# The first DFT of the last two x tiles by column block, and the order of the moves behind it

## The chip, the core and the metric

The kernel runs on one core of one Trainium2 chip. The metric is the device time of one execution in microseconds (us). The page of the profile and its trace come from one profiled execution of their own; its span runs from the first to the last instruction.

## The reference

Two layers follow each other on `x` of 4096 rows by 640 columns, both scaled and shifted by vectors made from `c` (`mod = silu(c) @ w_mod`, six vectors of 640). The change lies in the first layer, a spectral one; the second, a gated feed-forward layer with F = 1728, follows it in the same program.

```python
h = layernorm(x) * (1 + ca) + sa
X = rfft2(h)                     # along the 4096 rows: 2049 frequencies
z = X.reshape(..., 4, 160)       # 4 blocks of 160 columns
hr = relu(zr @ w1[0] - zi @ w1[1] + b1[0]);  hi = relu(zi @ w1[0] + zr @ w1[1] + b1[1])
o_r = hr @ w2[0] - hi @ w2[1] + b2[0];       o_i = hi @ w2[0] + hr @ w2[1] + b2[1]
y = irfft2(softshrink(o_r + 1j * o_i, 0.01))
x = x + ga * y
h = layernorm(x) * (1 + cb) + sb
x = x + gb * ((silu(h @ w_gate) * (h @ w_up)) @ w_down)
```

All is float32.

## The kernel before, in words

The 4096 rows are taken as 128 x 32 (`n1` on the partitions, `n2` in a tile's rows). The FFT is done in two steps of matrix products.

**First DFT, along n1.** Eight tiles `xa0` to `xa7` hold four values of `n2` each (128 partitions, 4 x 640). For each tile `ln_stats` (L379) takes mean and variance on VectorE and the inverse root on GpSimd, `ln_apply` (L390) normalizes the four rows, some on ScalarE and some on VectorE, `dft_a` (L408) multiplies with the constant `fa` on TensorE, and `evac_a` (L418) copies the products from PSUM back into `xa`. A product of 128 x 512 covers either one row's first 128 columns of all four blocks (`i` = 0 to 3) or the last 32 columns of all blocks and rows (`i` = 4, the remainder columns); they land in `xa[:, i, 0:512]` and `xa[:, :, 512:640]`. The loop at L431 runs these steps for t = 0 to 7, software pipelined: statistics two tiles ahead, normalization one.

**The turn through DRAM.** `moves` (L356) writes the tile to DRAM with `write_s1(t, f)` (L345), where f names which frequencies: f = 0 holds chunks 0 and 1 (32 of the 128 partitions, 320 KB), f = 1 chunks 2 and 3 (320 KB), f = 2 the last four chunks (640 KB). `load_g(ch)` (L301) reads a chunk back with `n2` on the partitions: `g` of chunk `ch`, 128 partitions (4 n2 + q) by 4 x 640, in four DMAs, one for each q. The first chunk is read in two parts: rows n2 < 28 from GpSimd's queue, the last four from SyncE's (SP's) queue after tile 7 is written. All other moves named here go through SP's queue, in program order; a DMA that waits there holds all behind it.

**Second DFT and the two layers, by chunk.** Eight chunks `ch` with four blocks `b` each make 32 steps p = 4 ch + b (L806). For a block, `stage_b(ch, t)` (L547, eight matmuls) makes the spectrum of columns 128 t to 128 t + 127 out of `g`; t = 0 to 3 are the blocks' first 128 columns, t = 4 the remainder columns of all four. `evac_b` (L555) splits a product into a high part (ScalarE) and a low part (VectorE), tile `z`; for chunk 0 `evac_r` (L568) does the same with the remainder columns of a block, tile `rz`. For later chunks the remainders go through DRAM: `rem_high`, `rem_low`, `rem_move`, `rem_read` (L600 to L622). `stage_l1` (L624) is the first complex layer, `tail_l1` (L661) its last part, `stage_l2` (L669) the second layer, `stage_i` (L729) the inverse step. In step p come `stage_l1(p)`, the `stage_b` of a later block, `stage_l2` of p - 1, `stage_i` of p - 7.

PSUM has eight banks: two each for the tags p1, p2, p3, and single ones b0 and b1. `stage_b` takes b0, for t = 4 b1 (L549); `stage_l2` takes p2. The bank b1 with chunk 0's remainders is read by `evac_r` of all four blocks, so `stage_b(1, 4)` can start only when the last of them is done.

**The weights.** `load_weights` reads raw w1 or w2 (two DMAs of 640 KB, `rm` and `rr`), `prep_weights` lists the jobs, `weights_high` (L278) rounds a weight to its high part and `weights_low` (L284, VectorE) makes the low part. For w1 the high parts are ScalarE's (L448), for w2 GpSimd's (L478). `first_scale` (L403) and `columns` (L316) make the vector `ca1` = 1 + ca; `idle(n)` (L324) issues 2 n small matmuls that compute nothing that is used.

**Memory.** The tiles of the pool `p2` (L468: w2a, w2b, w2c, tt and others) lie where the `xa` tiles lay, so each waits until the writes of the tile under it are done. Before the steps, L453 to L462 issue the second chunk's load, the writes of tiles 0 and 4 to 7 for f = 1, the third chunk's load, and those for f = 2.

The order is written out by hand: each engine runs its instructions in program order, and only semaphores hold it.

## Time and profile before

| | us |
|---|---|
| time, median of 3 runs | 1468.21 (1466.46 to 1470.22) |
| the profiled execution, its own time | 1461.29 |
| its span on the page | 1459.5 |
| TensorE busy in the span | 1416.4 |
| VectorE busy | 1083.6 |
| ScalarE busy | 785.5 |
| GpSimd busy | 551.7 |

The profiled execution was 6.92 us faster than the median of the three runs beside it. In the rows of the trace a timeline line gives start, length, engine, line of the kernel, operation, tiles written and read, shapes and a count; in brackets stands how long the engine was idle before it and what released it. PE is TensorE, PEld its weight loads, DVE VectorE, ACT ScalarE, POOL GpSimd, SPq SyncE's queue; for SPq and for DMA rows on POOL the length is that of the issue, not of the transfer.

### The profile page before, as it was taken

The page shows a single profiled execution, that of the slowest core. Times are in us where ns is not written, and L with a number is a line of the kernel's source. Part 1 is how long each engine was busy: PE and PEld are TensorE (multiplying, and loading weights), DVE is VectorE, ACT ScalarE, POOL GpSimd, SP SyncE. Part 2 cuts the span into 40 slices and gives each one's busy share as a digit, 9 for nine tenths or more (in the row PEclk, how much of TensorE's full clock was granted, in tenths as well). Part 3 has the DMA queues.
Part 4 walks back from the last instruction along what each step waited for, and adds up shares of the span by engine and source line. Part 5 has one row for each costly group of instructions (what it writes and reads, how often), then busy time and mean ns, then how long its engine had stood idle before and what let it go on. Part 6 is the DMA issues. An engine that isn't in the chain of part 4 may idle for free.

```text
span 1459.5 us, 24171 instructions
## 1 busy us (share of the span) xinstructions
PE 1416.4 (97%) x8628; PEld 1341.4 (92%) x8628; DVE 1083.6 (74%) x1963; ACT 785.5 (54%) x1554; POOL 551.7 (38%) x646
## 2 busy tenths in 40 slices
PE   6999999998999999999999999999999999999998
PEld 2799999966888888899999999999999999999998
DVE  8568877878797788757887768888747767567775
ACT  7658888744545555544565446555434444244432
POOL 5400100044655444322544424444324545046532
PEclk9999999999999999999999999999999999999999
DMA  9967767648677988798987997877696666966652
GB/s 379 338 215 228 232 199 219 220 145 275 235 276 267 337 293 279 274 364 291 314 271 248 342 367 254 310 246 249 237 345 219 222 215 238 352 212 232 205 188 83
DMA packets 184712, 380.07 MB, mean 260 GB/s; under 512 B 22480, under 2 KB 103056, under 8 KB 182544
## 3 DMA queue, kind: packets, MB, share of 16 engines
q1 hardware_dynamic: 176080, 360.99, 71.8%
q0 software_dynamic: 6928, 14.91, 3.3%
q10 hardware_dynamic: 1584, 2.62, 0.5%
q8 instruction: 68, 1.11, 0.3%
q14 instruction: 52, 0.43, 0.1%
HBM read 263.91 MB, written 105.39 MB: 253 GB/s over the span
## 4 chain that ended last, share of the span: by engine, by line
PE 61%; DVE 8%; DMA 4%; issue 2%; ACT 2%; POOL 1%; SPq 0%; POOLq 0%; DVEq 0%; ACTq 0%
PE pd L2269 12%; PE pw L1950 8%; PE pw L1948 8%; PE pw L1949 8%; PE pd_X L2129 4%; PE pg L1813 2%; PE pg L1812 2%; PE pg L1814 2%; PE pd_Y L2129 2%; PE pw L1959 2%; PE pw L1960 2%; PE pw L1961 2%; DMA cr<-s 2%; DVE wb L1266 2%; PE pd_Z L2129 1%
## 5 line engine op out<-in xcount | busy, mean ns | idle before, releaser
L2269 PE MATMUL pd<-wdh,a 128*128 128x320 f32 x1040 | 238.9, 310 | 1.5 <-DVE a L1849 1.3
L2269 PEld LDWEIGHTS pd<-wdh,a 128*128 128x128 f32 x1040 | 176.2, 188 | 2.5 <-DVE a L1849 1.6
L1266 DVE TENSOR_TENSOR wb<-r,wb 128x512 fp32r<-128x512 f32 (+3 forms) x156 | 159.8, 1032 | 16.3 <-ACT wb L1263 14.0
L2269 PE MATMUL pd<-wdl,a 128*128 128x320 f32 x540 | 166.3, 309 | 0.0
L1948 PE MATMUL pw<-h,wt 128*128 128x384 f32 x416 | 140.8, 339 | 3.1 <-ACT s_x L1967 2.1
L1950 PE MATMUL pw<-h,wt 128*128 128x384 f32 x416 | 140.4, 338 | 0.0
L1949 PE MATMUL pw<-h,wt 128*128 128x384 f32 x416 | 139.9, 336 | 0.0
L1263 ACT ACTIVATE wb<-r 128x512 fp32r<-128x512 f32 (+3 forms) x172 | 117.9, 703 | 32.8 <-PE pw L1961 24.8
L2241 DVE TENSOR_TENSOR x<-x,pd 128x320 f32<-128x320 f32 x240 | 108.9, 477 | 35.7 <-PE pd L2269 32.1
L1950 PE MATMUL pw<-h,wb 128*128 128x384 f32 x312 | 105.1, 337 | 2.3 <-DVE wb L1266 2.3
L1948 PE MATMUL pw<-h,wb 128*128 128x384 f32 x312 | 105.5, 338 | 0.0
L1949 PE MATMUL pw<-h,wb 128*128 128x384 f32 x312 | 105.0, 337 | 0.0
L1812 PE MATMUL pg<-ht,wb 128*128 128x512 f32 x260 | 102.8, 396 | 1.3 <-ACT wb L1263 1.3
L1814 PE MATMUL pg<-ht,wb 128*128 128x512 f32 x260 | 101.7, 391 | 2.2 <-DVE wb L1266 2.2
L2269 PEld LDWEIGHTS pd<-wdl,a 128*128 128x128 f32 x540 | 101.4, 188 | 0.5
L1813 PE MATMUL pg<-ht,wb 128*128 128x512 f32 x260 | 101.5, 390 | 0.0
L742 POOL DMA_DIRECT2D s<-co x28 | 15.5, 555 | 190.8 <-ACT co L741 183.0
L1967 ACT ACTIVATE s_x<-pw 128x384 f32<-128x384 f32 x52 | 25.4, 489 | 113.6 <-PE pw L1950 112.9
L1525 POOL TENSOR_TENSOR cr<-cr,gab 128x640 f32<-128x640 f32 x28 | 47.5, 1696 | 100.5 <-DMA cr<-s 89.6
L1948 PEld LDWEIGHTS pw<-h,wt 128*128 128x128 f32 x416 | 78.3, 188 | 4.7 <-ACT s_x L1967 3.1
L1949 PEld LDWEIGHTS pw<-h,wt 128*128 128x128 f32 x416 | 78.3, 188 | 0.0
L1950 PEld LDWEIGHTS pw<-h,wt 128*128 128x128 f32 x416 | 78.3, 188 | 0.0
(335 smaller groups left out, 4079.0 us busy)
## 6 DMA issues: line engine op xcount, KB each, us to landing
wt<-td SPq DMA_DIRECT2D x104, 512.0 KB, 5.3
hs<-ho SPq DMA_DIRECT2D x52, 512.0 KB, 5.5
h<-hs SPq DMA_DIRECT2D x32, 768.0 KB, 7.9
r<-in_B_w_gate_dram SPq DMA_DIRECT2D x36, 640.0 KB, 4.8
r<-in_B_w_up_dram SPq DMA_DIRECT2D x36, 640.0 KB, 5.0
wdr<-wdd SPq DMA_DIRECT2D x21, 640.0 KB, 5.2
td<-wt SPq DMA_DIRECT2D x25, 512.0 KB, 6.0
g<-s SPq DMA_DIRECT2D x28, 320.0 KB, 5.9
```

What stands on the lines that cost most here:

```text
L1263: act.activation(wbs[t, n][:, 0, ks, e], raw[t, n][:, ks, e], AF.Copy)
L1266: (pool if onp else dve).tensor_tensor(wbs[t, n][:, 1, ks, e], raw[t, n][:, ks, e], f32(wbs[t, n][:, 0, ks, e]), op=OP.subtract)
L1525: pool.tensor_tensor(crs[r], crs[r], gab, op=OP.mult)
L1812: mm(b, wh, hh, start=(kk == 0), stop=False)
L1813: mm(b, wh, hl, start=False, stop=False)
L1814: mm(b, wl, hh, start=False, stop=(kk == 4))
L1948: mm(b, w(0, kp), a[:, kp, 0], start=start and kp == 0, stop=False, skip_group_check=not start)
L1949: mm(b, w(0, kp), a[:, kp, 1], start=False, stop=False, skip_group_check=not start)
L1950: mm(b, w(1, kp), a[:, kp, 0], start=False, stop=kp == 1, skip_group_check=not start)
L2129: mm(bk[b, i][:, :320], x, y, start=new and j == 0, stop=j == len(seq) - 1, skip_group_check=not new)
L2241: dve.tensor_tensor(x2[:, e], x2[:, e], x[0][:, :320], op=OP.add)
L2269: mm(pd[g, hf][0][:, :320], l, m, start=i == 0, stop=i == len(s) - 1 and not (last and len(gs) > 1))
```

## The change

The tiles 0 to 5 go as before. For tiles 6 and 7 the DFT is taken by column block (`dft_c`, `evac_c`): product i < 4 holds block i's first 128 columns of all four rows, i = 4 the remainder columns, which now go to a tile `rst` of their own. Block 0 and the remainders of both tiles come first, are written (`first`) and read back for chunk 0; the other three blocks (`rest`) follow, with the raw weights w2 and the writes of tiles 2 and 3 for f = 1 and 2 between. All rows of tile 7 are normalized on VectorE, and three of tile 6. The high parts of w1 are made between the evacuations, `idle(54)` becomes `idle(14)`. Each part of `load_g` is one DMA instead of four. The other writes for f = 1 and 2 wait behind a small DMA (`s1h`) that reads the second chunk's tile. In the steps, only `stage_b(0, 0)` and `stage_b(0, 4)` stand ahead of the loop; blocks 1 and 2 come in step 0, block 3 in step 1. The high part of w2b moves from GpSimd to ScalarE (step 0), the low parts of w2 to the ends of step 0 and the middle of step 1, and chunk 1's `rem_move` and `rem_read` from SP's queue to GpSimd's.

```diff
-            def load_g(ch, lo=0, hi=32, dma=None):
+            def load_g(ch, lo=0, hi=32, dma=None, cols=(slice(0, D),)):
...
-                for q in range(4):
-                    (dma or nc.sync).dma_start(gs[ch][4 * lo + q:4 * hi:4], src[q, lo:hi])
+                for e in cols:
+                    (dma or nc.sync).dma_start(gs[ch][4 * lo:4 * hi, :, e], src[:, lo:hi, :, e].rearrange("q n j d -> n q j d"))
...
+                def write_s1(t, f, cols=None, dma=None):
+                    r = slice((0, 2, 1)[f], 128, (4, 4, 2)[f])
+                    if t < 6:
+                        (dma or nc.sync).dma_start(s1[f][:, 4 * t:4 * t + 4, :], xas[t][r])
+                        return
+                    for e in cols or (slice(0, 512), slice(512, 640)):
+                        (dma or nc.sync).dma_start(s1[f][:, 4 * t:4 * t + 4, e], rst[t][r] if e.start == 512 else xas[t][r, :, e])
...
-                        raws[2] = load_weights(rp, w2, "2")
-                    elif t < 7:
-                        if t == 6:
-                            load_g(0, 0, 28, pool)
+                    elif t == 4:
                         for f in (1, 2):
-                            write_s1(t - 3, f)
-                    else:
-                        load_g(0, 28, 32)
+                            write_s1(1, f)
+                    elif t == 5:
+                        load_g(0, 0, 20, pool)
...
-                        if i >= (4, 2, 2, 3, 2, 3, 2, 3)[t]:
+                        if i >= (4, 2, 2, 3, 2, 3, 1, 0)[t]:
...
+                def dft_c(t, i):
+                    xnr = xas[t].rearrange("p a (b e) -> p a b e", b=NB)
...
+                    mm(pa, fa, xnr[:, :, i, 0:128] if i < 4 else xnr[:, :, :, 128:160], start=True, stop=True)
+                    pas[t, i] = pa
+
+                def evac_c(t, i, eng=None):
+                    if i == 4:
+                        o = rst[t] = low_p.tile([P, 4, 128], F32, tag="e", bufs=2, name=f"rst{t}")
+                    else:
+                        o = xas[t][:, :, 128 * i:128 * i + 128]
+                    v = pas[t, i].rearrange("p (a e) -> p a e", a=4)
+                    if eng:
+                        eng.tensor_copy(o, v)
+                    else:
+                        act.activation(o, v, AF.Copy)
...
+                ln_apply(7)
+                for q in ((6, 0), (6, 4), (6, 1), (7, 0), (7, 4)):
+                    dft_c(*q)
+                evac_c(6, 0)
+                evac_c(6, 4)
+                evac_c(6, 1)
+                first_scale(0, 3)
+                evac_c(7, 0, dve)
+                evac_c(7, 4, dve)
+                first = (slice(0, 128), slice(512, 640))
+                rest = (slice(128, 512),)
+                write_s1(6, 0, first)
+                write_s1(7, 0, first)
+                load_g(0, 20, 32, None, first)
+                raws[2] = load_weights(rp, w2, "2")
+                for q in ((6, 2), (6, 3), (7, 1), (7, 2), (7, 3)):
+                    dft_c(*q)
+                jobs = prep_weights(raws[1], w1a, w1b, w1c, True)
...
+                for job in jobs[:3]:
+                    weights_high(*job)
+                evac_c(6, 2)
+                evac_c(6, 3)
+                evac_c(7, 1)
+                for job in jobs[3:6]:
+                    weights_high(*job)
+                evac_c(7, 2)
+                evac_c(7, 3)
+                for job in jobs[6:]:
+                    weights_high(*job)
+                write_s1(6, 0, rest)
+                write_s1(7, 0, rest)
+                for f in (1, 2):
+                    write_s1(2, f)
+                load_g(0, 20, 32, None, rest)
+                for f in (1, 2):
+                    write_s1(3, f)
+
+                first_scale(3, 5)
                 remainders(acc0, wx0)
                 pm1 = columns(acc0, wx0)
+                idle(14)
+                for job in jobs[:4]:
+                    weights_low(*job)
                 dve.tensor_scalar(ca1, pm1[:, 0:5], 1.0, None, op0=OP.add)
-                idle(54)
-                for job in prep_weights(raws[1], w1a, w1b, w1c, True):
-                    weights_high(*job)
+                for job in jobs[4:]:
                     weights_low(*job)
...
-            for t in (0, 4, 5, 6, 7):
-                write_s1(t, 1)
+            nc.sync.dma_start(s1h, gs[1][127:128, 3, 0:16])
+            for f in (1, 2):
+                for t in (0, 4, 5, 6, 7):
+                    write_s1(t, f)
             load_g(2)
             load_tb(2)
-            for t in (0, 4, 5, 6, 7):
-                write_s1(t, 2)
...
-            for job in prep2:
-                weights_high(*job, pool)
+            prep2 = [prep2[k] for k in (0, 3, 1, 4, 2, 5)]
+            for n, job in enumerate(prep2):
+                if n // 2 != 1:
+                    weights_high(*job, pool)
+            pool.dma_start(bm.rearrange("p a b c -> p (a b c)"), k_bm)
...
-                pb = bank0(1 if t == 4 else 0, [P, 2, 256], f"pb{ch}_{t}")
+                pb = (ps.tile([P, 2, 256], F32, tag="p2", name=f"pb{ch}_{t}") if (ch, t) in ((0, 1), (0, 3)) else
+                      bank0(1 if t == 4 else 0, [P, 2, 256], f"pb{ch}_{t}"))
...
-                nc.sync.dma_start(rzd[ch, :, :, 0:NN], f32(rts[ch].rearrange("p l i k -> p (l i) k")[:, :, 0:NN]))
+                (pool if ch == 1 else nc.sync).dma_start(rzd[ch, :, :, 0:NN], f32(rts[ch].rearrange("p l i k -> p (l i) k")[:, :, 0:NN]))
...
-            for b in range(3):
-                stage_b(0, b)
-                if b == 0:
-                    stage_b(0, 4)
-                evac_b(0, b)
-                evac_r(0, b)
-                if b == 1:
-                    idle(8)
-            for job in prep2[:3]:
-                weights_low(*job)
+            stage_b(0, 0)
+            stage_b(0, 4)
+            evac_b(0, 0)
+            evac_r(0, 0)
...
-                if b == 0:
+                if p < 2:
+                    todo = ([(0, 1), (0, 2)], [(0, 3), (1, 4), (1, 0)])[p]
+                elif b == 0:
                     todo = [(ch, 3)]
...
                     if q[1] < 4:
                         evac_b(*q)
+                        if q[0] == 0:
+                            evac_r(*q)
                 for f, *a in sums.get(p, ()):
                     f(*a)
-
                 if p == 0:
-                    evac_rh(0, 3)
+                    for job in prep2[2:4]:
+                        weights_high(*job)
+
+                if p == 1:
+                    for job in prep2[3:]:
+                        weights_low(*job)
...
-                if p == 0:
-                    evac_rl(0, 3)
...
                 if p == 0:
-                    for job in prep2[3:]:
+                    for job in prep2[:3]:
                         weights_low(*job)
```

33 lines of the change are left out of this document (16 added, 17 removed).

## The prediction, made before the change was run

> **What bounds the kernel now.** I read the page first, then the busy time in stretches, then TensorE's timeline of the first 110 us.
>
> ```profile
> span 1459.5 us, 24171 instructions
> PE 1416.4 (97%) x8628; PEld 1341.4 (92%) x8628; DVE 1083.6 (74%) x1963; ACT 785.5 (54%) x1554; POOL 551.7 (38%) x646
> ...
> 84.46:1459.50 1375.04, 1347.76 (x8302) 1296.04 (x8300) 1022.20 (x1800) 729.42 (x1454) 515.69 (x573) 1.00 0.75 255
> ...
> 63.60:84.46 20.86, 17.61 (x130) 17.23 (x131) 15.86 (x28) 12.37 (x26) 3.51 (x4) 0.92 0.78 298
> ```
>
> In a row of a stretch stand its length, the busy time of PE, PEld, DVE, ACT and POOL, the granted clock, the DMA share and GB/s. From 84.46 us on TensorE is busy for 98% of the time: whatever brings that point forward is kept to the end. The change acts before it.
>
> ```profile
> 31.24 17.74 PE L415 MATMUL pa<-xa,fa 128*128 128x512 f32 x40 [1.81 <-ACT xa L397]
> 49.67 1.05 PE L320 MATMUL pmc<-ones,acc 128*128 128x1 f32 x8 [0.69 <-ACT xa L426]
> 50.80 12.30 PE L327 MATMUL pz<-ones 128*128 128x128 f32 x108
> 63.61 2.02 PE L552 MATMUL pb<-tb,g 128*128 128x128 f32 x16 [0.50 <-DMA g<-s]
> ...
> 72.51 1.05 PE L552 MATMUL pb<-tb,g 128*128 128x128 f32 x8
> 74.11 0.40 PE L639 MATMUL pl<-rz,w1c 128*128 128x256 f32 x2
> ...
> 75.78 0.28 PE L652 MATMUL pl<-rz,w1c 128*128 128x256 f32 x1
> 78.63 3.22 PE L552 MATMUL pb<-tb,g 128*128 128x128 f32 x16 [2.56 <-DVE rz L592]
> 84.46 0.52 PE L639 MATMUL pl<-z,w1a 128*128 128x256 f32 x3
> 89.02 0.60 PE L685 MATMUL pc<-w2a,h 128*128 128x320 f32 x3
> 90.20 0.52 PE L639 MATMUL pl<-z,w1a 128*128 128x256 f32 x3
> 104.62 1.95 PE L552 MATMUL pb<-tb,g 128*128 128x128 f32 x16
> ```
>
> The last DFT ends at 31.24 + 17.74 = 48.98. Then TensorE multiplies nothing of use for 12.3 us (L327 is `idle`) and waits for `g`: the second DFT starts at 63.61. A second hole, 2.56 us, waits for VectorE's `rz` (bank b1). Step 2 starts at 84.46, step 3 at 90.20. So two stretches count: the trip through DRAM, and the chain from the first `stage_b` to step 2, 20.85 us long.
>
> **The trip through DRAM.**
>
> ```profile
> 39.30 11.77 SPq L346 DMA_DIRECT2D s<-xa  x10
> 54.54 5.46 SPq L309 DMA_DIRECT2D g<-s  x8
> ...
> 52.32 2.64 POOL L309 DMA_DIRECT2D g<-s  x4 [11.45 <-DMA s<-xa]
> ...
> xx<-tt SPq DMA_DIRECT2D x12, 160.0 KB, 3.0
> ...
> rzd<-rt SPq DMA_DIRECT2D x2, 512.0 KB, 6.1
> ...
> DMA to landing us min/median/max: 3.3/6.1/6.9
> ...
> 45.00:50.00 5.00, 4.31 (x13) 1.83 (x12) 0.98 (x2) 4.16 (x9) 0.00 (x0) 1.00 0.96 399
> ```
>
> Before, the last write goes out just before 51.07; the last load waits for its landing until 54.54 and lands some 6 us after its issue (the line "to landing" is of L309), because the DMA engines are full (share 0.96). The change takes 1.31 MB of raw weights and two of three 0.98 MB writes out of the queue ahead of that point: 3.3 MB, at 0.40 MB per us 8 us of transfers, so by 43 us the queue has run empty.
>
> ```profile
> 40.20 0.61 DVE L395 TENSOR_SCALAR xa<-xa,mv_a,rs_a 128x640 f32<-128x640 f32 x1 [0.93 <-POOL rs_a L197]
> 41.31 3.65 DVE L406 SCALAR_TENSOR_TENSOR acc<-wm,sc,acc 128x640 f32<-128x640 f32 x4
> 49.02 1.29 DVE L422 COPY xa<-pa 128x512 f32<-128x512 f32 x2 [4.06 <-PE pa L415]
> ...
> 40.73 2.10 ACT L426 ACTIVATE xa<-pa 128x512 f32<-128x512 f32 x4
> ```
>
> *Ends of the DFT.* 20 products in 17.74 us are 0.887 each; the last ten start at 40.1 and end at 48.98 in either order, the fifth (tile 7's remainders) at 44.6. ScalarE has one 128x640 pass less (about 0.8) ahead of tile 5's five copies and ends them at 42.5, not 43.3; three copies of 2.10 / 4 are done at 44.1. VectorE normalizes tile 7 from 40.2 (four times 0.54, to 42.4), adds three terms of `first_scale` (0.55 and two of 0.91, to 44.7) and copies two products (1.29): 46.0. TensorE keeps 48.98, as all this lies beside it; so do w1's high parts, twelve passes of at most 0.63 (a row below) and about 5 us in all, done by 52 and wanted after 55.
>
> *First part.* The last write is issued at 46.1, against 50.6 (51.07 less one issue). An empty queue lands a small DMA in about 3.0 (row of xx), so at 49.1; the two loads are issued at 49.1 and 49.7 (5.46 / 8 = 0.68 each) and land by 52.7 to 53.0 (3.0 to 3.3). TensorE: the columns from 49.0 (1.1 us), then 28 matmuls of 12.30 / 108 = 0.114: 3.2, so it is free at **53.4**, and that is the first `stage_b`, 10.2 us earlier. The load is covered by `idle` with 0.4 to 0.7 us to spare; past that each us late costs one.
>
> *Second part.* On SP's queue the weights follow at 50.3, then two writes `rest` (0.39 MB), (2, 1) and (2, 2), 0.98 MB. At 0.42 MB per us from 51.6 the weights end at 54.7, `rest` at 55.7 and lands at 56.7. Only then does SP issue the load of `rest`; behind 2.3 us of writes, to 58.0, its 0.29 MB land at about **60.0** (3.3 after the issue, the minimum of L309's row). Bounds: 59.3, the end of these transfers, and 66, if the write's landing takes the 3.5 of before (51.07 to 54.54) and the load the crowded 6.9. I take the near end, since the ring is emptier. TensorE wants it 5.85 us after its first `stage_b`: two of them 2.02, ScalarE's and VectorE's `rz` 1.9 (rows below), and what of `stage_l1` follows its first product with `rz`, 1.8 (74.11 to 75.9). That is 59.3, so it is late by 0.7.
>
> That a load of some columns waits for those columns alone: the trace lets ScalarE write strided columns of `w1a` while VectorE has not yet written the others that the program lists earlier.
>
> ```profile
> 52.81 0.63 ACT L282 ACTIVATE w1a<-rm 128x512 fp32r<-128x512 f32 x1
> ...
> 53.01 0.29 DVE L285 SCALAR_TENSOR_TENSOR w1a<-rm,w1a 128x128 fp32r<-128x128 f32 x1
> ```
>
> **The chain from `stage_b(0, 1)` to step 2.** This is where the change gives back.
>
> ```profile
> L592 DVE SCALAR_TENSOR_TENSOR rz<-pb,ca,rz 32x256 fp32r<-32x256 f32 x8 | 3.9, 483 | 0.9 <-ACT rz L582 0.8
> L560 DVE SCALAR_TENSOR_TENSOR z<-pb,ca,z 128x512 fp32r<-128x512 f32 x5 | 3.7, 747 | 11.2 <-ACT z L559 11.2
> ...
> L285 DVE SCALAR_TENSOR_TENSOR w2b<-rm,w2b 128x640 fp32r<-128x640 f32 x2 | 1.6, 818 | 0.0
> L644 DVE TENSOR_TENSOR h<-h,h 128x256 fp32r<-128x256 f32 x4 | 1.5, 419 | 0.0
> L657 DVE SCALAR_TENSOR_TENSOR u<-pl,b1r,u 64x256 f32<-64x256 f32 x2 | 1.0, 476 | 0.1
> ...
> L665 DVE SCALAR_TENSOR_TENSOR r<-u,r 64x256 fp32r<-64x256 f32 x2 | 0.8, 418 | 0.1
> ...
> L559 ACT ACTIVATE z<-pb,ca 128x512 fp32r<-128x512 f32 x12 | 8.3, 689 | 16.8 <-PE pb L552 16.8
> L582 ACT ACTIVATE rz<-pb,ca 32x256 fp32r<-32x256 f32 x8 | 3.7, 467 | 0.3 <-PE pb L552 0.2
> ...
> L722 ACT ACTIVATE xh<-xx 128x640 fp32r<-128x640 f32 x3 | 2.2, 729 | 0.0
> ```
>
> Before, blocks 0 to 2 were split while TensorE idled. Now, from 60.0: block 1 on TensorE 1.05, to 61.1. ScalarE: z and rz of blocks 1 and 2, two times 0.69 + 2 x 0.47, to 64.4 with overlaps; the two high parts of w2b, not shown on ScalarE, by the same shape in L722 0.73 each (bounds 0.69, the smaller z, and 1.8, POOL's), to 65.8; the tail of `stage_l1(0)`, as long as VectorE's (L665), to 66.2. VectorE: its tail 0.42; three low parts of w2, 0.75 pipelined, to 68.9; the low parts of `stage_l1(1)` (L644 twice, L657, pipelined) 1.15; z and rz of block 3, 0.75 + 0.97, to 71.8. Only now is b1 free for `stage_b(1, 4)`: TensorE has stood from about 66.5, 5.3 us. With `stage_b(1, 0)` that takes 3.22 at the slow rate of 78.63 (bounds 1.95, row of 104.62, and 3.9, twice that): 75.0. z(1, 0), which the program puts ahead of the last low parts: ScalarE 0.69, VectorE 0.75, 76.5; three low parts of w2, 2.3, to 78.8; the last product and the second half of `stage_l2(0)` (89.02 to 90.20, 1.18) 1.5: step 2 starts at **80.4**. Against 84.46 that is 4.0 us less, and counted the other way: 10.2 won, 5.85 + 20.4 - 20.85 = 5.4 given back in the longer chain, 0.7 to the late second part.
>
> The other edits cost nothing while covered. POOL's w2a and w2c wait for raw weights and for the writes of tile 3, which land by 62 (0.98 MB behind the load of `rest`); they are needed from 66.6 and 77. The second chunk, 1.31 MB behind those, lands near 66, wanted at 71.8. The bulk writes behind `s1h`, 4.9 MB or 11.7 us, free the memory of tt by 77, wanted at 79. Chunk 1's remainders on POOL's queue are issued at 80.5; nothing is queued behind them there until step 7. A landing of 6.1 (row of rzd), four issues of 0.68 and a landing of 3.0 to 3.3 end near 92, wanted at 93.
>
> **The clock.**
>
> ```profile
> 80.00:81.00 1.00, 1.00 (x7) 0.50 1.02 401
> 82.00:83.00 1.00, 1.00 (x7) 0.65 1.05 442
> ```
>
> The third number from the end is the granted clock: after the hole of 2.56 us it stood at 0.50 and came back within the stretch 82 to 83. That is in the 3.22 above. A second such stretch may follow the 2 us of waiting inside `stage_l2(0)`; on three us of work it costs some 1.5 and leaves 2.5 of the 4.0 (1465.7, within the forecast's range). I take none, since that wait is shorter than the one that the trace shows. The Trainium skill, "TensorE: Matmul & The Clock Gate", section "HAM oscillation", gives as a rule that gaps of more than some 3.4 us slow the clock. The trace has it after 2.56, so the measurement decides; by that page the new 5.3 us hole costs one slow stretch and the 2 us could not bring a second.
>
> **The rivals.** (a) No slow clock, second part in time: 0.7 and 1.3 less, 78.4, 6.0 us gained: 1462.2. For it: the slow window may fall into the hole. (b) The second part lands 2 to 4 us later, at 62 to 64: the gain shrinks to 2 to 0, about 1467.2. For it: 1.31 MB of weights lie right ahead of it. (c) Slower: the second part lands at 66, its upper bound, because its write and its load each wait in a queue that the weights and (2, f) have filled. The gain is gone from 64.0 on; at 66 step 2 starts at 86.4, and TensorE, having stood for 6 us ahead of block 1, pays another slow stretch of 1.7: 3.6 us slower, 1471.8. Against it: the queue is empty at 49. (d) The change doesn't do what it says: `stage_b(0, 0)` waits for both parts. Then the first `stage_b` is at 60.0 and step 2 follows 5.85 + 20.4 later: 86.3, 1.8 us slower, 1470.0. The two rows of w1a speak against it.
>
> **How the numbers follow.** The profiled execution takes 1461.29; 4.0 less is 1457.3. The median of the runs is 1468.21, 6.9 above it; I predict on that: **1464.2**. Forecast 0.46 (a gain of 2 to 5), (a) 0.20, (b) 0.14, (c) 0.15, (d) 0.05. The range leaves out a tenth on each side: 1460.0 (gain of (a), and 2 us of spread of the runs, 1466.46 to 1470.22) to 1472.0 (case (c)). The forecast's own range is 1463 to 1466.5. A measurement of this kernel can tell about 0.3%, 4.4 us, from no change. Faster by more: all of (a) and 0.21 of the forecast, 0.41. Slower by more: 0.08 of (c), 0.02 of (d) and 0.02 of the rest, 0.12. Within: 0.47.
>
> **What would show it.** In the profile after: `pz` 28 matmuls long and the first `stage_b` near 53.4; the second near 60, released by DMA g; a hole of 5 us before `stage_b(1, 4)`, released by DVE rz; step 2 near 80.4; after it TensorE as busy as before. A first `stage_b` beyond 55, a second beyond 64, or TensorE waiting for `rz` by DMA in step 4 would make the prediction wrong.

## The result and the profile after

The changed kernel takes 1472.58 us (median of 17 runs), the kernel before 1466.46 (17 runs beside them): **1.0043 times as long, 95% interval 1.0032 to 1.0054**, some 6 us slower. Predicted were 1464.2, 4.0 less than the 1468.21 it started from. The profiled execution takes 1473.94 us. Executions of one kernel differ by several us (the 17 of before ran from 1461.96 to 1470.22), so the start is compared below by the traces and the whole by the ratios.

"Step n" is the n-th pass of the main loop; it begins with its first product `pl<-z,w1a`. First the page of after and its busy time in stretches (length; busy PE, PEld, DVE, ACT, POOL; granted clock; DMA share; GB/s).

```profile
span 1472.1 us, 23954 instructions
PE 1415.9 (96%) x8532; PEld 1338.0 (91%) x8532; DVE 1082.6 (74%) x1967; ACT 782.5 (53%) x1552; POOL 549.9 (37%) x646
```

```profile
90.52:1472.10 1381.58, 1350.81 (x8301) 1296.94 (x8300) 1018.65 (x1798) 728.08 (x1454) 518.61 (x578) 1.00 0.74 253
55.55:90.52 34.97, 23.15 (x115) 21.69 (x115) 16.53 (x29) 13.72 (x28) 8.92 (x8) 0.70 0.96 343
```

From step 2 on TensorE is as busy as before (98%), though the stretch lasts 6.5 us longer than in the profiled execution of before (1375.04 us). The stretch ahead of it grew from 20.86 to 34.97 us, with more than 11 us of holes and a mean clock of 0.70 instead of 0.92. TensorE's timeline shows the holes, in brackets with what ended them:

```profile
49.74 3.37 PE L328 MATMUL pz<-ones 128*128 128x128 f32 x28
55.55 3.51 PE L615 MATMUL pb<-tb,g 128*128 128x128 f32 x16 [2.44 <-DMA g<-s]
...
67.18 3.78 PE L615 MATMUL pb<-tb,g 128*128 128x128 f32 x16 [3.98 <-DMA g<-s]
...
80.37 3.75 PE L615 MATMUL pb<-tb,g 128*128 128x128 f32 x16 [4.97 <-issue]
...
90.52 0.84 PE L702 MATMUL pl<-z,w1a 128*128 128x256 f32 x3
...
97.53 0.51 PE L702 MATMUL pl<-z,w1a 128*128 128x256 f32 x3
```

The three lines L615 begin with `stage_b` of (0, 0), of (0, 1) and of (1, 4); each holds a second one, (0, 4), (0, 2) and (1, 0). For the hole of 4.97 us the profile names no releaser; VectorE's `rz` of block 3 ends at 80.27, 0.1 us ahead, and e4 below shows that it is the bank. Beside the prediction:

| start of, us | before | predicted | after |
|---|---|---|---|
| first `stage_b` | 63.61 | 53.4 | 55.55 |
| `stage_b(0, 1)` | 66.30 | 60.0 | 67.18 |
| step 2 | 84.46 | 80.4 | 90.52 |
| step 3 | 90.20 | 86.1 | 97.53 |
| step 5 | 102.10 | 98.0 | 109.01 |

(Predicted steps 3 and 5 are 80.4 and the length that the steps had before.) Step 5 is 6.9 us late, and the medians differ by 6.1. The two profiled executions differ by another 5.7 us behind step 5: from there to the end of the span it takes 1357.4 us in before and 1363.1 in after. The kernel before shows both values by itself: a second trace of it (e12) has 1358.0, and e16, changed only ahead of the first `stage_b`, 1363.1. So three terms are to be explained: the second part (7.2 us later than predicted), the chain behind it (23.3 us instead of 20.4) and step 2 itself (7.0 instead of 5.7). The issues on the DMA queues between 42 and 53 us, and then between 54 and 70 us (number, KB of one, median us from issue to landing):

```profile
g<-s POOLq DMA_DIRECT2D x1, 800.0 KB, 9.6
...
s<-xa SPq DMA_DIRECT2D x2, 64.0 KB, 8.7
s<-rst SPq DMA_DIRECT2D x2, 64.0 KB, 7.6
```

```profile
rm<-in_A_w_dram SPq DMA_DIRECT2D x1, 640.0 KB, 4.3
rr<-in_A_w_dram SPq DMA_DIRECT2D x1, 640.0 KB, 6.4
...
s<-xa SPq DMA_DIRECT2D x2, 192.0 KB, 6.4
```

The first part's four writes (64 KB each) took up to 8.7 us to land, not 3.0, and those of the second part 6.4. The load on GpSimd's queue landed at 52.1 (issued at 42.47), the last of the four writes at 52.6. Meanwhile the DMA engines were far from full. The last column but one is their share, first in the kernel before, then in after; the work that didn't run between 44 and 56 us keeps them full until 96:

```profile
44.00:48.00 4.00, 4.00 (x11) 1.74 (x10) 0.93 (x2) 4.00 (x8) 0.00 (x0) 1.00 1.01 425
48.00:52.00 4.00, 3.31 (x23) 2.48 (x22) 2.44 (x6) 3.15 (x7) 0.00 (x0) 1.00 0.92 383
52.00:56.00 4.00, 4.00 (x38) 4.00 (x37) 4.00 (x11) 3.08 (x10) 3.60 (x6) 1.00 0.84 271
...
92.00:96.00 4.00, 4.00 (x33) 4.00 (x32) 2.72 (x6) 2.46 (x6) 0.00 (x0) 1.00 0.61 141
```

```profile
44.00:48.00 4.00, 4.00 (x11) 1.85 (x10) 3.93 (x7) 3.56 (x9) 0.00 (x0) 1.00 0.74 181
48.00:52.00 4.00, 4.00 (x33) 3.52 (x32) 3.90 (x10) 3.65 (x10) 0.00 (x0) 1.00 0.55 135
52.00:56.00 4.00, 1.56 (x13) 1.40 (x13) 0.95 (x4) 0.00 (x0) 0.00 (x0) 0.98 0.26 63
...
92.00:96.00 4.00, 4.00 (x30) 4.00 (x29) 1.30 (x3) 2.67 (x7) 0.00 (x0) 0.83 1.03 339
```

### The profile page after: what moved, and what is told of

Read it like the earlier page. It is cut to its first block, busy times and chain, and to the rows that moved or that the text cites. A ratio compares the mean times of both kernels' runs of the same rounds, so it can differ in the third digit from the quotient of the medians.

```text
span 1472.1 us, 23954 instructions
## 1 busy us (share of the span) xinstructions
PE 1415.9 (96%) x8532; PEld 1338.0 (91%) x8532; DVE 1082.6 (74%) x1967; ACT 782.5 (53%) x1552; POOL 549.9 (37%) x646
## 4 chain that ended last, share of the span: by engine, by line
PE 61%; DVE 6%; DMA 5%; issue 2%; ACT 2%; POOL 2%; SPq 0%; ACTq 0%; POOLq 0%; DVEq 0%
PE pd L2332 12%; PE pw L2013 8%; PE pw L2011 8%; PE pw L2012 8%; PE pd_X L2192 4%; PE pg L1875 2%; PE pg L1876 2%; PE pg L1877 2%; PE pd_Y L2192 2%; PE pw L2022 2%; PE pw L2024 2%; PE pw L2023 2%; DMA hs<-ho 2%; DMA cr<-s 2%; PE pd_Z L2192 1%
## 5 line engine op out<-in xcount | busy, mean ns | idle before, releaser
L2013 PEld LDWEIGHTS pw<-h,wt 128*128 128x128 f32 x416 | 78.1, 188 | 0.0
```

Of the source, the lines that this page charges most:

```text
L2013: mm(b, w(1, kp), a[:, kp, 0], start=False, stop=kp == 1, skip_group_check=not start)
```

## The experiments

**Theories.** *Moves*: the first part's writes wait for chunk 0's load of 20 rows, the second's for the raw weights ahead of them. *Chain*: from `stage_b(0, 1)` on, VectorE's order and bank b1 set the pace. Rivals: GpSimd's queue, or pieces of 512 bytes, are slow by themselves; TensorE's halved clock is the cause. Later came a fourth theory, *dates*: the bulk transfers set a date further on, so that what is won at the start is lost there. e1 to e4, e8, e9 and e11 change one thing in the changed kernel (e11 besides has e1's edit); e7 starts from the kernel before. All ratios are to the kernel before, run beside them. By their whole time none of e1 to e4, e6, e8 and e9 can be told from the changed kernel (1.0032 to 1.0054); what each term costs is read from the traces, one execution each. e13 and e18 lie below its interval.

| kernel | first `stage_b` | `stage_b(0, 1)` | step 2 | step 5 | ratio (95%) |
|---|---|---|---|---|---|
| e1, load on SP | 56.31 | 68.22 | 90.4 | 108.1 | 1.0054 (1.0039 to 1.0069) |
| e2, 16 rows | 52.97 | 64.32 | 86.9 | 105.3 | 1.0060 (1.0044 to 1.0077) |
| e3, weights behind | 56.65 | 64.38 | 86.2 | 106.7 | 1.0040 (1.0024 to 1.0055) |
| e4, other bank | 56.08 | 67.77 | 86.5 | 106.5 | 1.0041 (1.0025 to 1.0056) |
| e6 = e2 + e3 + e4 | 52.67 | 59.78 | 79.1 | 103.0 | 1.0030 (1.0018 to 1.0042) |
| e7, before, moves alone | 59.23 | 61.93 | 80.6 | 105.8 | 1.0041 (1.0028 to 1.0055) |
| e8, no early load | 53.38 | 66.17 | 89.5 | 108.3 | 1.0042 (1.0028 to 1.0056) |
| e9, holes filled | 56.84 | 69.00 | 90.9 | 109.9 | 1.0066 (1.0045 to 1.0088) |
| e10 = e7 + bulk writes first | 58.93 | 61.85 | 81.6 | 100.6 | 1.0007 (0.9997 to 1.0017) |
| e11, 17 rows | 77.73 | 89.82 | 113.2 | 131.6 | one run, 1489.84 us |
| e12, before again | 63.62 | 66.31 | 84.5 | 102.5 | 1.0006 (0.9992 to 1.0021) |
| e13 = e6 without `s1h` | 53.06 | 59.53 | 78.1 | 102.3 | 1.0014 (0.9998 to 1.0030) |
| e14, before, other bank | 64.17 | 66.86 | 83.0 | 103.1 | 0.9997 (0.9982 to 1.0011) |
| e15 = e10 + other bank | 59.53 | 62.23 | 78.8 | 101.9 | 0.9996 (0.9982 to 1.0010) |
| e16, before, started later | 69.37 | 72.00 | 90.2 | 108.1 | 1.0030 (1.0018 to 1.0042) |
| e17 = e15, chunk 2 later | 59.77 | 63.39 | 80.2 | 102.3 | 1.0006 (0.9989 to 1.0024) |
| e18 = e13, chunk 2 later | 53.73 | 59.94 | 79.0 | 102.1 | 1.0003 (0.9983 to 1.0023) |
| e19 = e15, chunk 2 on POOL | 59.08 | 61.77 | 79.6 | 100.5 | 0.9990 (0.9974 to 1.0006) |

(In e7, e10, e12, e14 to e17 and e19, built on the kernel before, the block (0, 1) is the third `stage_b` and follows the first at once.)

**The first part: e1, e2, e8, e11.**

```diff
-                        load_g(0, 0, 20, pool)
+                        load_g(0, 0, 20)            # e1
+                        load_g(0, 0, 16, pool)      # e2; the two later loads from row 16
+                        load_g(0, 0, 17)            # e11; the two later loads from row 17
+                                                    # e8: no such line; the later loads from row 0
```

> The changed kernel, with the load of chunk 0's rows below 20 issued from SP's queue instead of GpSimd's. Queue theory: the four small writes of the first part land at 51.8 to 52.6, six to nine us after their issue, because GpSimd's load of 0.8 MB holds the DMA engines from 44 to 50.6. In SP's queue that load is done before them, in about 3 us: they land by 49.5, the first stage_b starts at 53.2 (the end of idle) instead of 55.55, all that follows in SP's queue is 3 us earlier, the second part lets TensorE go at 64 instead of 67.2, step 2 starts at 87 to 88 instead of 90.5, and the time is 3 us below the changed kernel's. Rival, small pieces: writes in pieces of 512 bytes are slow by themselves; then they land past 51.5 here too, and nothing is gained. Chain theory: the first stage_b may come earlier, but step 2 moves by less than half of that.

> The changed kernel, with chunk 0 cut at row 16 instead of 20: GpSimd loads 16 rows, the two later parts hold 16 instead of 12. If the slowness of GpSimd's load is that of a DMA whose row count has only 10 as a divisor up to 16, it now runs at full width: done by 48.5 instead of 50.6, small writes landed by 49.5 to 50, first stage_b at 53.2 to 53.5, step 2 at 88 to 88.5, 2 us below the changed kernel. If the cause is GpSimd's descriptors as such, the writes still land after 51 (a fifth fewer bytes: 1.3 us earlier at most) and step 2 stays within 1.5 us of 90.5.

> Chunk 0's early load of 20 rows is left out; all 32 rows come with the two column loads. Queue theory (the first part's small writes land late since the load on the other queue holds the DMA engines): the writes land at 49.0 to 49.8 instead of 51.8 to 52.6, the load of 0.33 MB by 53.5, first stage_b 53 to 54 instead of 55.55. The second part has 0.98 MB to load instead of 0.37: stage_b(0, 1) at 68.5 to 71, step 2 at 91 to 94, the time 1 to 3 us above the changed kernel's: ratio 1.004 to 1.007. Rival (pieces of 512 bytes are slow by themselves): the writes land at 51.5 or later as in the changed kernel.

> Chunk 0 cut at row 17 in place of 20, its load on SP's queue as in e1. If a load is spread over as many DMA engines as divide its rows (16 for 16, 10 for 20, 1 for 17): 272 pieces of 2560 bytes one after the other on one engine, at 0.1 to 0.2 us each 27 to 55 us, first stage_b at 72 to 100 and the time 20 to 45 us above the changed kernel's. If the rows don't matter: landing in 7 to 9 us as in e1, first stage_b at 55 to 58, time as e1.

DMA issues of e1 (42 to 54 us), e8 (42 to 60 us) and e2 (40 to 53 us); then e11's first `stage_b` and two stretches of its trace:

```profile
s<-xa SPq DMA_DIRECT2D x2, 64.0 KB, 8.0
s<-rst SPq DMA_DIRECT2D x2, 64.0 KB, 7.0
```

```profile
s<-xa SPq DMA_DIRECT2D x2, 64.0 KB, 2.0
s<-rst SPq DMA_DIRECT2D x2, 64.0 KB, 1.9
```

```profile
g<-s POOLq DMA_DIRECT2D x1, 640.0 KB, 8.0
...
s<-xa SPq DMA_DIRECT2D x2, 64.0 KB, 6.2
s<-rst SPq DMA_DIRECT2D x2, 64.0 KB, 4.8
```

```profile
77.73 3.75 PE L615 MATMUL pb<-tb,g 128*128 128x128 f32 x16 [23.71 <-DMA g<-s]
```

```profile
52.00:56.00 4.00, 2.03 (x19) 1.83 (x17) 1.87 (x6) 0.57 (x3) 0.00 (x0) 1.00 0.07 26
56.00:60.00 4.00, 0.00 (x0) 0.00 (x0) 0.00 (x0) 0.00 (x0) 0.00 (x0) 0.73 0.06 26
```

With the load on SP's queue the writes behind it are as late (8.0): it isn't GpSimd's queue. Without the load the same small writes land in 2.0 us: it isn't their pieces. So they wait behind the load: in e2, too, they land by 49.8, right behind the load at 49.1. And what the load costs hangs on its number of rows: 17 rows in SP's queue (e1 had 20 there) leave a DMA share of 0.06 to 0.07, one engine's sixteenth, and TensorE stands for 23.7 us. The Trainium skill, "DMA: Bandwidth & Descriptors", section "Why a DMA increments its semaphore by 16 and not by 1", says that a transfer is spread over the largest number of engines up to 16 that divides the slowest dimension of both sides. By that rule 17 rows get 1 engine, 20 rows 10 and 16 rows 16. e11 agrees. The shares of 0.74 and 0.55 in after, with other moves beside the load, neither show nor exclude ten engines of sixteen (0.63). e2, with 16 rows, brings the first `stage_b` to 52.97, 2.6 us earlier; that the engine count makes those 2.6 us isn't shown, since e2's load is also smaller and was issued 1.4 us earlier, and it still took 8.0.

**The second part: e3.**

```diff
-                raws[2] = load_weights(rp, w2, "2")     # ahead of the second dft_c loop
...
                 load_g(0, 20, 32, None, rest)
+                raws[2] = load_weights(rp, w2, "2")
```

> The changed kernel, with the raw weights w2 loaded behind the second part's load instead of ahead of the second part's writes. Queue theory: the writes of the second part, issued at 55.5 and landed at 62.0 to 62.5, now go out at 54.5 and land at 58; its load lands at 61.5 to 62.5; TensorE, which ended stage_l1 at 63.2 and stood until 67.2, goes on at once; step 2 starts at 86 to 87 instead of 90.5, and the time falls by 4 us. Rival: the weights come late instead (landing 65 to 66), GpSimd's high parts of w2a are done at 69 and of w2c at 73, and as VectorE needs them only after 71 and 82, they cost nothing; if they do cost, step 2 stays at 89 or later, with TensorE or VectorE released by GpSimd's w2.

Issues of e3 between 54 and 70 us:

```profile
rm<-in_A_w_dram SPq DMA_DIRECT2D x1, 640.0 KB, 6.1
...
s<-xa SPq DMA_DIRECT2D x2, 192.0 KB, 2.4
```

The writes of the second part land in 2.4 us instead of 6.4, and `stage_b(0, 1)` is 2.8 us earlier, although the first part was 1.1 later. The weights ahead of the second part cost some 4 us.

**The chain and the clock: e4, e9.**

```diff
# e4
-                pb = (ps.tile([P, 2, 256], F32, tag="p2", ...) if (ch, t) in ((0, 1), (0, 3)) else
+                pb = (ps.tile([P, 2, 256], F32, tag="p2", ...) if (ch, t) in ((0, 1), (0, 3)) else
+                      ps.tile([P, 2, 256], F32, tag="p3", ...) if (ch, t) == (1, 4) else
# e9: idle(14) -> idle(32), and ahead of two stage_b
                 for q in todo:
+                    if q in ((0, 1), (1, 4)):
+                        idle(28 if q[0] == 0 else 36, "p3")
                     stage_b(*q)
```

> The changed kernel, with stage_b(1, 4) in a bank of the tag p3 instead of b1, which holds chunk 0's remainders until VectorE has split block 3's. Chain theory: the hole of 5 us before stage_b(1, 4) goes (67.2 to 75.4 without a stop), z(1, 0) is split at 81 instead of 85.6, the last low parts of w2 end at 83.3, step 2 starts at 85 to 86 instead of 90.5, and the clock is back earlier: 4 to 6 us below the changed kernel, about the time of before. Queue theory alone: what ends last is the transfers, and step 2 stays within 1 us of 90.5.

> The changed kernel with idle products in the three holes: 32 for 14 before the first stage_b, 28 before stage_b(0, 1), 36 before stage_b(1, 4). Clock theory (the half clock after the holes costs 2.9 us in the chain and 1.2 in step 2): the time at half clock falls from 24 us to under 10, stage_b(0, 1) stays near 67, step 2 comes at 87 to 88.5 instead of 90.5, step 3 6 us later; 3 to 4 us less in all, ratio 1.001 to 1.003. Rival (VectorE and ScalarE set the chain, whatever TensorE's clock): step 2 at 89.5 or later and step 2 alone is shorter; 1.0035 or more.

TensorE's waits of e4 in the timeline, then two lines of e9's and its stretch from the first `stage_b` to step 3:

```profile
67.77 3.78 PE L616 MATMUL pb<-tb,g 128*128 128x128 f32 x16 [5.53 <-DMA g<-s]
...
82.41 0.64 PE L749 MATMUL pc<-w2b,h 128*128 128x320 f32 x1 [4.27 <-DVE w2b L286]
```

```profile
75.67 8.20 PE L328 MATMUL pz<-ones 128*128 128x128 f32 x72
83.70 1.95 PE L615 MATMUL pb<-tb,g 128*128 128x128 f32 x16
```

```profile
56.84:96.65 39.81, 35.44 (x289) 34.02 (x288) 19.70 (x36) 16.78 (x35) 8.99 (x8) 1.00 0.93 329
```

In e4 the hole ahead of `stage_b(1, 4)` is gone, 4.27 us of it reappear one stage on (VectorE's low parts of w2), and the chain is 18.7 instead of 23.3. Part of that can be the clock, which stood at half from 79.72 to the end of the chain in after and in e4 only from 82.00. In e9 the granted clock is 1.00 throughout, and still step 2 comes no earlier: by the expectation the rival won. But the fills were sized wrongly: one `idle` makes two products, so that 36 of them last 8.2 us and TensorE starts `stage_b(1, 4)` at 83.70, 2.6 us after VectorE's `rz` of block 3 had ended. What e9 does tell is the price of the clock: from `stage_b(1, 4)` to step 2 it takes 7.2 us instead of 10.15, step 2 takes 5.7 instead of 7.0. That is 2.9 + 1.3 = 4.2 us. Its ratio is no better, since the fills cost as much: the first `stage_b` is 1.3 us later than in after, (0, 1) 1.8, (1, 4) 2.6 later than it could be.

**All undone together, and the moves alone: e6, e13, e7, e10.** e6 is e2, e3 and e4 in one; e13 leaves out the `s1h` line besides. e7 makes the reordering in the kernel before, without column blocks; e10 adds the changed kernel's order of the bulk writes and its queue for chunk 1's remainders.

```diff
# e7, in moves(t) of the kernel before; idle(54) -> idle(25); one DMA for each load_g
-                        raws[2] = load_weights(rp, w2, "2")
...
+                    elif t == 5:
+                        load_g(0, 0, 16, pool)
+                    elif t == 7:
+                        load_g(0, 16, 32)
+                        raws[2] = load_weights(rp, w2, "2")
+                        ...                              # then write_s1(2, f), write_s1(3, f)
# e10, besides
-            load_g(2)                                    # and load_tb(2): now behind the next two lines
             for t in (0, 4, 5, 6, 7):
                 write_s1(t, 2)
```

> Chunk 0 cut at row 16, raw weights behind the second part's load, stage_b(1, 4) in another bank: the three undone together. If the two late moves and the chain are the whole cause, their shares add: first stage_b near 53, stage_b(0, 1) at 59.5 to 61, step 2 at 78 to 80 (59.5 plus the 18.7 that the other bank gave), step 5 at 98.5 to 100.5, held up only by chunk 1's remainders (some 2 us of waiting in step 4). That is 8 to 10 us ahead of the changed kernel and 2 to 3 ahead of the one before: 0.997 to 1.000 of its time, with 1 to 2 us lost to the later small waits that all kernels with the change showed. Rival: what the change costs lies behind step 5 and doesn't depend on the start; then the ratio stays at 1.003 or above although step 5 is early.

> The three changes of e6 and, besides, without the s1h move, so that the bulk writes no longer wait for chunk 1. In e6 step 4 waited 4.7 us for chunk 1's remainders, whose write into rzd took 10.3 us to land beside the bulk writes (issued 68.8 to 81.2, landed by 88.8). If those writes on the DMA engines are the cause: issued from 57 on they land by 80 to 82, rzd lands in 6 us, the wait in step 4 falls below 1.5 us, step 5 starts at 98 to 100 instead of 103.0, and the time is 3 to 5 us below e6: ratio 0.999 to 1.001. If the trip of the remainders is late for a reason of its own (GpSimd's queue): the wait stays above 3 us, the ratio at 1.002 to 1.004.

> The kernel before with the order of the moves alone: writes of tiles 2 and 3 and the raw weights behind chunk 0's load, which is cut at row 16 and made in one DMA each, and 25 idle products for 54; no column blocks, order of stage_b and splitting as before. If the gain of the moves was real and the loss lies in the split by columns and in the longer chain: first stage_b at 56 to 58, step 2 some 21 later, at 77 to 79, 5 to 7 us ahead of before; ratio 0.995 to 0.998. If a load in large pieces is slow whatever is in the queue (8 us as in the changed kernel): the load of the last rows is issued at 51 and lands at 59, first stage_b at 59 to 60, 0.997 to 1.000. If the moves themselves are the loss: 61 or later, 1.000 or more.

> As e7 (before with the order of the moves alone), with the second half of the bulk writes ahead of chunk 2's load and chunk 1's remainders on GpSimd's queue, as in the changed kernel. In e7 VectorE waited 7.4 us for the memory of tt (writes of s<-xa landing up to 88.4) and TensorE 5.0 behind it. If that wait is all that kept e7 from its gain: tt at 82 to 84, step 3 at 87 to 89 instead of 93.6, step 5 at 99 to 102, ratio 0.998 to 1.001. Rival (every order of the moves misses one of the dates, since the DMA engines are full to 90 us and the trip leaves them empty for some us): another wait of 3 us or more takes its place (chunk 1's remainders or chunk 2), step 5 at 103 or later, ratio above 1.002.

One line each: e6's `rz` of step 4 on TensorE, e13's, and VectorE's `tt` in e7.

```profile
96.38 0.47 PE L703 MATMUL pl<-rz,w1c 128*128 128x256 f32 x2 [4.67 <-DMA rz<-rzd]
```

```profile
95.27 0.76 PE L702 MATMUL pl<-rz,w1c 128*128 128x256 f32 x2 [4.83 <-DMA rz<-rzd]
```

```profile
88.61 0.49 DVE L690 TENSOR_TENSOR tt<-pc,b2t 128x320 f32<-128x320 f32 x1 [7.39 <-DMA s<-xa]
```

The shares add as expected: e6 reaches step 2 at 79.1, 11.4 us ahead of the changed kernel and 5.4 ahead of before. But step 5 is at 103.0: in step 4 TensorE stands 4.7 us for chunk 1's remainders. e13's bulk writes went out some 4 us earlier (the last at 77.00 instead of 81.19), and the wait was the same 4.8: it wasn't those writes alone that held them. Nor did the time follow the start: e6 is at 1.0030 with step 5 only 0.9 us behind before, so its rival, a cost behind step 5, isn't excluded by it; e13 is at 1.0014. In e6, e13 and e18 TensorE also waits 2.5 to 3.2 us ahead of `stage_b(1, 4)`, released by the DMA of chunk 1's table `tb`, which stands in SP's queue behind chunk 1's load: with the bank's wait gone, this date takes its place. In e7 VectorE waits 7.4 us for the memory of `tt`, which the last bulk writes hold, and step 3 comes at 93.6 instead of 86. With these ahead (e10) that wait is gone and step 5 is at 100.6, but step 4 waits for the remainders again, 1.5 us.

**Which date holds: e14, e15, e17, e18, e19, and two controls, e12 and e16.** e14 and e15 put `stage_b(1, 4)` in another bank, as e4, in the kernel before and in e10. The last three move chunk 2's load:

```diff
-            load_g(2)
-            load_tb(2)
...
                 if b == 2 and ch + 1 < NCH:
                     rem_read(ch + 1)
+                if p == 2:
+                    load_g(2)              # e17 on e15, e18 on e13; in e19 load_g(2, dma=pool)
+                    load_tb(2)
```

> The kernel before with one edit: stage_b(1, 4) writes another bank, so that it no longer waits 2.56 us for VectorE's rz of block 3. If that wait is worth what it lasts: stage_b(1, 4) at 76, no stretch at half clock at 79.3, step 2 at 81 to 82.5 (w2's low parts end at 80.9), 2 to 3.5 us less: ratio 0.998. If the next date takes it back (memory of tt released by the bulk writes at 85.7, chunk 1's remainders wanted in step 4): step 2 early, but step 3 or step 5 at 89.5 and 101.5 or later, ratio 0.9993 to 1.0005.

> e10 with the same edit. There the hole ahead of stage_b(1, 4) was 3.6 us. If the edit is worth that: step 2 at 78.5 to 79.5 instead of 81.6, step 5 at 98.5, ratio 0.997 to 0.999, faster than both kernels. If the DMA engines set the pace (bulk writes to 85.3, remainders' read in step 4): step 4 waits 3 to 5 us for rz in place of 1.5, step 5 at 100 to 101, ratio 1.000 to 1.001.

> As e15, with chunk 2's load (1.31 MB) and its table issued behind the read of chunk 1's remainders in place of ahead of the loop. In every kernel so far the remainders landed between 94.8 and 97.4, whether their write had been issued at 78 or at 87.6, while the DMA engines were full up to some 90. If that load is what they waited behind: the engines are through with the bulk writes by 85 to 86, rz has landed by 90 to 91.5, the wait of 4.0 us in step 4 falls below 1, step 5 at 97 to 98.5 instead of 101.85 and chunk 2 lands by 95, wanted at 98: ratio 0.996 to 0.998, faster than both kernels. If another transfer or the remainders' own trip sets the date: rz still lands at 94 or later, or chunk 2 is late, step 5 at 101 or later, ratio 0.999 to 1.001.

> As e13 (the changed kernel with cut at 16, weights behind, other bank, no s1h), with chunk 2's load behind the read of chunk 1's remainders. If the load was what the remainders waited behind: the wait of 4.8 us in step 4 falls below 1.5, step 5 at 97 to 98.5 instead of 102.3, 4 to 5 us below e13: ratio 0.997 to 0.999. If not: as e13, 1.0014 within 0.0015.

> In e17 the load of chunk 2 was still issued at 80.05, ahead of the remainders, since SP's queue doesn't wait for GpSimd's. Here it is issued on GpSimd's queue, behind the read of the remainders, so that it can't be ahead of them. If it was what they waited behind: rzd issued at 81 to 83 lands by 87 instead of 89.7 to 90.2, rz by 90.5 to 91.5 instead of 95.1 to 95.5, the wait in step 4 is under 1 us, step 5 at 97 to 98.5 and chunk 2 lands near 95: ratio 0.996 to 0.998. If the rz move still lands at 94 or later, or chunk 2 comes too late for step 5: 0.999 or more, and the date is set by something else.

TensorE's first product with chunk 1's `rz` in step 4: before, e14, e15, e17, e18, e19.

```profile
97.00 0.47 PE L639 MATMUL pl<-rz,w1c 128*128 128x256 f32 x2 [0.17 <-issue]
```

```profile
98.02 0.47 PE L640 MATMUL pl<-rz,w1c 128*128 128x256 f32 x2 [1.45 <-DMA rz<-rzd]
```

```profile
95.23 0.72 PE L643 MATMUL pl<-rz,w1c 128*128 128x256 f32 x2 [4.04 <-DMA rz<-rzd]
```

```profile
95.62 0.48 PE L641 MATMUL pl<-rz,w1c 128*128 128x256 f32 x2 [3.00 <-DMA rz<-rzd]
```

```profile
95.62 0.77 PE L700 MATMUL pl<-rz,w1c 128*128 128x256 f32 x2 [3.08 <-DMA rz<-rzd]
```

```profile
93.83 0.48 PE L641 MATMUL pl<-rz,w1c 128*128 128x256 f32 x2 [1.83 <-DMA rz<-rzd]
```

Step 4 began at 90.3 to 91.8 in all but the first two (96.0 and 95.7), and yet this product comes at 95 to 98 in every one but e19 (e6, e10 and e13, too). That is the date. In e14 the hole of 2.56 us of the kernel before is gone and step 2 is 1.5 us earlier, but VectorE then waits 2.4 us for `tt` and TensorE for `rz`, and the time stays (0.9997). e17 and e18 failed as tests: SP's queue doesn't wait for GpSimd's, and it issued chunk 2's load at 80.05 and 83.5, still ahead of the remainders' read. Only e19 puts it behind, and there the product is 1.4 us earlier than in e15 and step 5 too (one trace each); so the load seems to be a part of what held them, not all: with the write issued at 81.8 and two landings to wait for, one behind the other, the trip itself takes 12 us. e19 is the fastest version that I ran, but 0.9990 (0.9974 to 1.0006) doesn't show it faster than the kernel before; against the changed kernel's 1.0043 it is.

> The kernel before once more, for a second trace. If the 2 us by which all kernels with the change are slower than their start explains belong to the one profiled execution of before (1461.29, with TensorE at full clock in all but 3.4 us before step 5): this execution shows some of those later waits too, and its step 5 lies at 102 to 104. If they belong to the change: all groups of waits behind step 5 are as in the first trace, within 1 us.

> The kernel before with 84 idle products for 54 and nothing else: the first stage_b starts 2.9 us later, at 66.5. It tells whether a shift of the start comes out one for one at the end. If it does: 2.5 to 3.5 us slower, ratio 1.0017 to 1.0024. If the later stretches answer to any shift with small waits of their own, as the kernels with the change suggest: 5 us or more, 1.0033 and above. If DMA dates and not TensorE's start set step 2: under 1.5 us, below 1.001.

e16 only makes TensorE idle longer (`idle(54)` to `idle(84)`); by the same slip as in e9 the start moved by 5.8 us, not 2.9. Step 5 moved by 6.0 and the time by 1.0030, 4.4 us (2.6 to 6.2): so four tenths or more of a shift of the start come out at the end, and one for one is within the interval. e12 shows the kernel before with step 5 at 102.5. The changed kernel's 6.9 us at step 5 and 6.1 us at the end agree with that. In e2 and e6 the time is some 5.6 and 3.5 us above the shift of step 5, in the others built on the changed kernel (without e11, a single run) 0 to 2. For e2 the traced execution is an odd one: it took 1464.29 us, 7.1 less than the median of its five. The later waits differ from execution to execution; whether the change has a share in them stays open.

## Why the prediction was wrong

- *What bounds the kernel*: right in the main. From step 2 on TensorE is as busy as before, and the shift of step 5 (6.9 us) is the result (6.1) within the spread of the executions. Step 2 was predicted at 80.4 and came at 90.52: the 10.1 us between are 7.2 of the second part and 2.9 of the chain.
- *First part*: this is the step that failed, "An empty queue lands a small DMA in about 3.0 (row of xx), so at 49.1", with "by 43 us the queue has run empty" ahead of it. GpSimd's queue held chunk 0's load of 20 rows, issued at 42.5, which the prediction had not put into the sum at all. The writes behind it land by 52.6, 3.5 us late, and the first `stage_b` is at 55.55 instead of 53.4. Without that load (e8) they land in 2.0 us and the first `stage_b` is at 53.38: for an empty queue the term was right.
- *Second part*: 67.18 instead of 60.0. Some 4.2 us come from that late start (the weights were issued at 54.51, not 50.3), 1.6 from the writes behind them (6.4 us to landing; e3: 2.4), 1.3 from the load (4.6 instead of 3.3). The near end was taken "since the ring is emptier"; it lies beyond even the far end, 66. The 5.85 us ahead of it, whose three terms as given add up to 5.7, measured 7.65 (55.55 to 63.20), with the clock at half for 3.4 of them; that cost nothing, as the second part was later still.
- *Chain*: 23.3 instead of 20.4. The order was right: the hole ahead of `stage_b(1, 4)` is 4.97 us (predicted 5.3), the second wait is in `stage_l2(0)`. The size of the clock was not: one stretch of 1.3 us was counted, and e9 prices the clock at 2.9 in the chain's last part and 1.3 in step 2. Without the 2.6 us that its fill came too late, e9's chain at full clock is 19.3; the predicted one without its 1.3 is 19.1.
- *Column split, the other edits at nothing*: right. `stage_b(0, 0)` did not wait for the second part (rival d), and none of the other edits shows up as a wait in after.
- *Rivals*: (c) named the right direction and half its cause, the weights in front. The argument against it, "the queue is empty at 49", is the same false step. Its 1471.8 lies near the measured 1472.58 by luck: it stands for 3.6 us more than the 1468.21 known then, and measured were 6.1 more than the 1466.46 of the runs beside it.
- *Signs*: two that it named came, a first `stage_b` beyond 55 and a second beyond 64. The third, TensorE waiting for `rz` by DMA in step 4, didn't come in after, where step 4 is late (103.28), but in every version whose step 4 began before 95.
- *What the gain is worth*: even with the second part at 59.8 and step 2 at 79.1, ahead of the prediction (e6), there is no gain. "Wanted at 93" against "near 92" for chunk 1's remainders was seen as met, but it is a date that holds back every version with an early start. No version that I ran, with the change or with its moves alone, won the 4 us, and none is shown faster than the kernel before.

## What to carry to other kernels

Taking transfers out of a full queue doesn't shorten them: ask which later date each of them had, and list these dates (here w2, the memory of `tt`, chunk 1's remainders) before counting a gain at the front. A small write that TensorE waits for must have nothing large issued ahead of it, neither on its own queue nor on another (e1 and after); and the row count at which a load is cut belongs into the sum (17 rows against 16 and 20). If TensorE is given holes on the way, put their slow clock into the sum for all the work that follows up to a stretch without waits, not for the first stage alone.

## What the runs showed of the hardware

- A load of 17 rows ran on a sixteenth of the DMA engines (share 0.06, 26 GB/s) and held the writes queued after it: the first took 29.2 us to land, 16.2 of them for its issue.
- The load of 16 or 20 rows took 8.0 to 9.6 us though it carries 0.64 to 0.8 MB; at the 0.40 MB per us of the full engines that would be 1.6 to 2. Why it is so slow with engines standing free isn't settled.
- Around the hole of 4.97 us the granted clock stood at half from 79.7 to 93.4, through work with waits of 0.6 to 1.0 us in it; in the kernel before, after 2.56 us, from 79.3 to 82.7. And a hole of 2.44 us, the one ahead of the first `stage_b`, was enough to halve it. The Trainium skill, "TensorE: Matmul & The Clock Gate", section "HAM oscillation", names gaps of more than some 3.4 us; here shorter ones do.
- Not every such hole does: after 2.63 us in e15, 2.73 in e7 and 2.74 in e3 the first `stage_b` ran at full clock (e15's line is below). The traces show what decides. In all twenty every stretch between two changes of the clock lasts a multiple of 3.41 us (in after 3.41, 6.83, 6.83, 6.83 and 13.65), so the changes lie on a grid of 3.41 us, which lies elsewhere from trace to trace. Between 53 and 105 us, in the 18 traces with a change there, the full clock fell to half after every interval of this grid in which TensorE stood for 1.83 us or more in all, and after none with 1.80 or less; it came back only after intervals with under 0.7 us. e15's 2.63 us fell into two intervals, with 0.83 and 1.80 us. So what a hole costs depends also on where the grid cuts it. Below are four intervals of after (length, busy PE, and the granted clock as the last number but two), then e15's first `stage_b` and its two intervals:

```profile
52.42:55.83 3.41, 0.97 (x9) 0.81 (x8) 0.53 (x3) 0.00 (x0) 0.00 (x0) 1.00 0.23 62
55.83:59.24 3.41, 3.41 (x18) 3.41 (x17) 0.75 (x1) 0.83 (x2) 0.22 (x1) 0.50 0.98 294
86.55:89.96 3.41, 2.78 (x9) 2.38 (x10) 2.91 (x5) 0.00 (x0) 0.14 (x1) 0.50 0.93 287
89.96:93.38 3.42, 3.42 (x17) 3.42 (x17) 0.49 (x1) 0.84 (x2) 0.63 (x1) 0.50 1.04 322
```

```profile
59.53 2.02 PE L556 MATMUL pb<-tb,g 128*128 128x128 f32 x16 [2.63 <-DMA g<-s]
```

```profile
54.32:57.73 3.41, 2.58 (x24) 2.39 (x22) 2.12 (x6) 1.02 (x4) 0.00 (x0) 1.00 0.87 197
57.73:61.15 3.42, 1.62 (x14) 1.65 (x15) 0.00 (x0) 0.46 (x1) 0.15 (x1) 1.00 1.00 344
```
